# Attention with a soft cap and two MoE layers: a fixed order for three engines in the first seven pairs

## The chip, the cores and the metric

One core of a Trainium2 chip runs the kernel. The metric is the device time of one execution in microseconds. An execution of the kernel before took 789.97 us as the median of three (789.9 to 790.86). The profile comes from one further execution, which took 788.29 us.

## The reference

Three steps are chained; the output of each is the input of the next. All is float32.

```
# 1. attention: 4 batches, 12 heads, 448 positions, head size 64
s = cap * tanh((q @ k.T / 8) / cap)                     # cap = 30
p = exp(s - max(s));  attn = p / (sum(p) + 1e-9) @ v
x = attn with the heads side by side                    # 1792 tokens x 768

# 2. first "MoE" layer: w_in 768 x 1024, w_out 1024 x 768
h = x @ w_in;  e = exp(h - max(h))
solu = h * e / (sum(e) + 1e-9)
y = ((solu - mean) / sqrt(var + 1e-6) * g_ln) @ w_out

# 3. second layer: 8 experts, top 1, w1 768 x 1024 and w2 1024 x 768 for each
logits = y @ w_gate + modality_bias[modality_id]
out = gate * (relu(y @ w1[e]) @ w2[e])                  # e, gate of each token
```

`w_in` and `w_out` come to the chip as 64-bit floats and are turned into 32-bit floats there.

## The kernel before, in words

**Attention.** The heads are worked on two at a time: six pairs (`p`) in each of the four batches (`b`), 24 pairs in a row. A pair has its keys in four chunks of 112. Each pair is two **half pairs** (`cp` 0 and 1) of two chunks. For the first eight pairs (`plain`) a half pair is: scores on TensorE (`sc`, L664), a tanh and an exp of each chunk on ScalarE (`e`, L667 and L669), then the products with v (`av`, L714) and, for the first six pairs, the row sums through TensorE (`S`, L720). TensorE adds the products of a pair's first two chunks in its second half pair, and those of the last two in the first half pair of the next pair; then `av` is copied to `X` (L729). Later pairs split k and q into a high and a low part (`a_split`, L645 to L648) and use these.

**Weights of the first MoE.** While the attention of batch 0 runs, `w_in` and `w_out` are brought in and converted block by block: 12 half rows of `w_in` (128x512) and 16 of `w_out` (128x384). GpSimd issues the load of a raw block (`conv_load`, L450; four buffers, so each load waits until an earlier block has been read). VectorE turns the raw bits into float32 in three operations (`f64_to_f32`, L426 to L428). A block of `w_in` is then split into a high part on ScalarE (L463) and a low part on VectorE (L464). A block of `w_out` is multiplied by `g_ln` (`g_t`) and split on VectorE (L478, L479), transposed on TensorE (`conv_tr`, L486, copied back by ScalarE, L488), and each full row of `w_out` is multiplied by `w_gate` (`conv_og`, L494 to L496), so that the logits come out of the same product as y. The list `CUS` says in which half pair a block is due: two in each of half pairs 0 to 13. Before, all `w_in` blocks came first, then all of `w_out`.

**First MoE.** When a batch is through, its row sums are turned into reciprocals (`a_fin1`: the sums are copied from PSUM, L733, turned round by TensorE, L737, inverted by VectorE, L739 to L742, transposed back, L744, and copied to `rh`, L745 and L746), spread over the heads by products with `sel` (`a_fin2`, `rb`, L751), and multiplied onto `X` (L753). Then the token tiles of the batch are pushed onto a list of steps (`msteps`: `h` products L536 to L538, the softmax of solu, transposes, `y` products L586 to L588). `fill` takes steps from the list between the parts of each later half pair, at a pace (`pace`) that should use the list up by the time when the next batch is pushed. Each half pair has three such fills, with shares `FW` that sum to 3.

**Second layer.** Behind the attention come the routing, one expert's block as soon as its tokens are known, and the rest of the experts in slots.

**Order of the work.** TensorE's order is the order of the program text in this whole part (`manual_schedule` with TensorE alone). The order of ScalarE, VectorE, GpSimd and the DMA queue SP is chosen by the framework's planner: it takes what it expects to be ready, with the program order as the priority. Waits between engines are on semaphores, and each engine executes its own list strictly in order. The scores, transposes and gate products of this part take their PSUM tiles from one pool of three (`atile`).

Of the kernel before, what the change touches and what calls it, by code (L numbers as in the profile page):

```python
# [10 lines left out]
F32 = mybir.dt.float32  # L11
# [31 lines left out]
TAIL = (12, 12, 10)  # L43
# [6 lines left out]
NRAW = 4  # L50
NTM = 4
# [10 lines left out]
FIN = (0, 1, 2, 2)  # L62
LEFT = (6, 6, 4)
RHA = 1
BIN = 0
# [17 lines left out]
def attn_moe_kernel(ctx, tc, qt, kt, vv, cap, w_in, w_out, g_ln, ids, w_gate, mbias, w1, w2, out):  # L83
# [50 lines left out]
    def setup_tables(tp):  # L134
        flat = tp.tile([P, NP, S], F32, tag="X", name="tmp").rearrange("p a b -> p (a b)")
# [12 lines left out]
        dve.tensor_add(sel, tmp, tmp2)  # L148
# [5 lines left out]
        pool.iota(pi, pattern=[[0, 1]], base=0, channel_multiplier=1, allow_small_or_imprecise_dtypes=True)  # L154
        pi2 = tm[:, 13:14]
# [5 lines left out]
        it = tm[:, 32:60].bitcast(I32).rearrange("p (t w) -> p t w", w=2)  # L161
        sp.dma_start(out=it, in_=ids)
        mb = tm[:, 64:80].rearrange("p (t w) -> p t w", w=NE)
        sp.dma_start(out=mb, in_=mbias)
# [10 lines left out]
        sp.dma_start(out=g_t, in_=g_ln)  # L175
        sp.dma_start(out=wg_t, in_=w_gate)
        zr = flat[0:1, 2 * NP * P + 256:2 * NP * P + 256 + YW]
        dve.memset(zr, 0.0)
        sp.dma_start(out=ysc[0:1, :], in_=zr)
# [250 lines left out]
    later = {0: [], 1: [], 2: []}  # L430

    def defer(pos, f):
        if pos < 0:
            f()
        else:
            later[pos].append(f)

    def deferred(pos):
        while later[pos]:
            later[pos].pop(0)()  # L440
# [3 lines left out]
    wraw = []  # L444

    def conv_load():
        if len(wraw) < len(blocks):
# [4 lines left out]
            wraw.append(raw)  # L452

    def conv_in(k, hf):
        raw = wraw[2 * k + hf]
# [14 lines left out]
    def conv_out(c, hf):  # L470
        HW_ = DM // 2
        raw = wraw[2 * ND + 2 * c + hf]
# [7 lines left out]
        wT[c, hf] = tf  # L480

    def conv_tr(c, hf):
        tf = wT[c, hf]
        pt = atile(f"pt{c}_{hf}")[:, 0, :]
        for i in range(3):
            pe.transpose(pt[:, i * P:(i + 1) * P], tf[:, i * P:(i + 1) * P], ident)  # L486
        tt = mp.tile([P, 3, P], F32, tag="x3", name=f"wT{c}_{hf}", bufs=4)
        act.copy(tt, pt[:, :3 * P].rearrange("p (a b) -> p a b", a=3))  # L488
        wT[c, hf] = tt
# [923 lines left out]
```

## Time and profile before

| | |
|---|---|
| median of three executions | 789.97 us |
| the profiled execution | 788.29 us |
| its span, first to last instruction | 786.6 us |
| TensorE busy | 737.2 us, 94% |
| VectorE busy | 452.6 us, 58% |
| ScalarE busy | 393.7 us, 50% |
| GpSimd busy | 209.8 us, 27% |
| mean granted TensorE clock | 0.980 |

Busy times of TensorE are modelled, since its matmuls are pipelined: two neighbours overlap in the records, and the distance of their starts is the time that one of them costs. "PE" is TensorE's matmul side and "PEld" its weight loads, "DVE" is VectorE, "ACT" ScalarE, "POOL" GpSimd, "SP" the queue that issues most loads. `L664` is line 664 of the kernel before. The granted clock is 1.00 at 2.4 GHz and falls by halves of time: a mean of 0.8 means that the clock was at 1.2 GHz for 40% of the stretch.

### The profile page before, as it was taken

To read this page: it belongs to the slowest core of one execution; us is meant where nothing else is said; L and a number is where in the kernel's file an instruction comes from. 1 tells how busy PE (TensorE), PEld (TensorE's weight loads), DVE (VectorE), ACT (ScalarE), POOL (GpSimd) and SP (SyncE) were. 2 spreads that over 40 slices of the span, in tenths; PEclk is the share of its full clock that TensorE was granted. 3 is DMA by queue.
4 is the path that set the end of the run, shared out by engine and by line. 5 is a ranking of instruction groups with operands and counts; after the bars stand their busy time and mean duration, and the time that the engine had idled before them with its cause. 6 is when DMAs were issued, how large, how long until landed. Compare 5 with 4: busy or idle time off the path is not lost.

```text
span 786.6 us, 11389 instructions
## 1 busy us (share of the span) xinstructions
PE 737.2 (94%) x4150; PEld 576.3 (73%) x4150; DVE 452.6 (58%) x833; ACT 393.7 (50%) x541; POOL 209.8 (27%) x285
## 2 busy tenths in 40 slices
PE   6889899998999998999999999899999999999993
PEld 2234456776677777676868799889879988799982
DVE  5987767767656665665444745747246163463630
ACT  5987656774656554556641223525136162553530
POOL 4222015352343351336432213540300211002010
PEclk9999999999999999999999999999999999999997
DMA  9856202231313221122000402476938459574620
GB/s 299 284 178 168 90 19 82 67 109 54 102 36 102 79 69 60 57 69 79 13 21 20 142 21 91 128 277 218 362 135 251 147 173 379 199 254 166 211 79 23
DMA packets 39060, 104.50 MB, mean 133 GB/s; under 512 B 6439, under 2 KB 16689, under 8 KB 38994
## 3 DMA queue, kind: packets, MB, share of 16 engines
q1 hardware_dynamic: 32466, 74.26, 29.0%
q0 software_dynamic: 6528, 29.42, 10.8%
q8 instruction: 34, 0.56, 0.3%
q14 instruction: 32, 0.26, 0.1%
HBM read 92.58 MB, written 11.27 MB: 132 GB/s over the span
## 4 chain that ended last, share of the span: by engine, by line
PE 78%; DVE 7%; issue 6%; ACT 3%; DMA 3%; POOL 1%; SPq 0%; POOLq 0%; DVEq 0%; ACTq 0%
PE av L714 8%; PE h L536 5%; PE y L586 5%; PE h L538 5%; PE y L588 5%; PE y L587 5%; PE h L537 5%; PE sc L689 3%; PE sc L690 3%; PE poD L1160 3%; PE poD L1161 3%; PE poD L1162 3%; PE phD L1091 3%; PE phD L1092 3%; PE phD L1093 3%
## 5 line engine op out<-in xcount | busy, mean ns | idle before, releaser
L692 ACT ACTIVATE e<-sc,sc 112x896 f32<-112x896 f32 x64 | 64.6, 1009 | 83.4 <-PE sc L690 81.2
L714 PE MATMUL av<-e,v 112*64 112x448 f32 x384 | 82.0, 560 | 3.1 <-ACT e L669 2.3
L586 PE MATMUL y<-wouh,lh 128*128 128x388 f32 x224 | 77.4, 345 | 2.2 <-ACT lh L576 1.9
L588 PE MATMUL y<-wouh,ll 128*128 128x388 f32 x224 | 76.4, 341 | 0.3 <-DVE ll L577 0.2
L587 PE MATMUL y<-woul,lh 128*128 128x388 f32 x224 | 76.2, 340 | 0.0
L536 PE MATMUL h<-winh,xh 128*128 128x512 f32 x168 | 69.3, 413 | 0.1
L538 PE MATMUL h<-winh,xl 128*128 128x512 f32 x168 | 66.8, 398 | 0.9 <-POOL xl L524 0.5
L693 ACT ACTIVATE e<-e,cap_t 112x896 f32<-112x896 f32 x64 | 66.9, 1045 | 1.5
L537 PE MATMUL h<-winl,xh 128*128 128x512 f32 x168 | 66.5, 396 | 0.0
L714 PEld LDWEIGHTS av<-e,v 112*64 112x64 f32 x384 | 24.9, 140 | 53.1 <-issue 38.4
L689 PE MATMUL sc<-qs,kh 128*112 128x448 f32 x128 | 48.2, 377 | 2.3 <-DVE u L548 1.3
L701 POOL TENSOR_TENSOR es<-es,e 112x448 f32<-112x448 f32 x32 | 40.8, 1276 | 34.1 <-DVE es L700 33.5
L586 PEld LDWEIGHTS y<-wouh,lh 128*128 128x128 f32 x224 | 42.4, 189 | 8.4 <-issue 4.3
L648 POOL TENSOR_TENSOR kl<-kr,kh 128x448 fp32r<-128x448 f32 x22 | 28.3, 1288 | 75.3 <-DVE kh L645 44.9
L690 PE MATMUL sc<-qs,kl 128*112 128x448 f32 x128 | 47.7, 372 | 0.0
L1037 DVE TENSOR_TENSOR wl_H<-raw_H,wh_H 128x768 fp32r<-128x768 f32 (+1 forms) x28 | 29.2, 1068 | 29.4 <-ACT wh_H L1036 29.3
L1037 DVE TENSOR_TENSOR wl_D<-raw_D,wh_D 128x768 fp32r<-128x768 f32 (+1 forms) x28 | 29.8, 1071 | 24.6 <-ACT wh_D L1036 24.0
L588 PEld LDWEIGHTS y<-wouh,ll 128*128 128x128 f32 x224 | 42.2, 188 | 1.1 <-DVE ll L577 1.0
L587 PEld LDWEIGHTS y<-woul,lh 128*128 128x128 f32 x224 | 42.3, 189 | 0.9
L1160 PE MATMUL poD<-wh_D,hhD 128*128 128x384 f32 x128 | 43.0, 336 | 0.0
L1162 PE MATMUL poD<-wh_D,hlD 128*128 128x384 f32 x128 | 42.8, 334 | 0.0
L1161 PE MATMUL poD<-wl_D,hhD 128*128 128x384 f32 x128 | 42.8, 334 | 0.0
(382 smaller groups left out, 1769.0 us busy)
## 6 DMA issues: line engine op xcount, KB each, us to landing
kr<-in_kt_dram SPq DMA_DIRECT2D x64, 112.0 KB, 2.5
qr<-in_qt_dram SPq DMA_DIRECT2D x64, 112.0 KB, 2.6
rawc<-in_w_in_dram POOLq DMA_DIRECT2D x12, 512.0 KB, 5.8
rawc<-in_w_out_dram POOLq DMA_DIRECT2D x16, 384.0 KB, 3.8
raw_D<-in_w_dram SPq DMA_DIRECT2D x12, 512.0 KB, 3.9
wr_T<-in_w_dram SPq DMA_DIRECT2D x16, 384.0 KB, 5.7
raw_D<-in_w_dram SPq DMA_DIRECT2D x16, 384.0 KB, 4.5
wr_T<-in_w_dram SPq DMA_DIRECT2D x12, 512.0 KB, 9.0
```

The lines of the kernel that those rows point to most:

```text
L536: pe.matmul(o, s["xh"][d], winh[d][:, c], start=(d == 0), stop=False)
L537: pe.matmul(o, s["xh"][d], winl[d][:, c], start=False, stop=False)
L538: pe.matmul(o, s["xl"][d], winh[d][:, c], start=False, stop=(d == ND - 1))
L586: pe.matmul(o, s["lh"][f], wouh[f][:, c], start=(f == 0), stop=False)
L587: pe.matmul(o, s["lh"][f], woul[f][:, c], start=False, stop=False)
L588: pe.matmul(o, s["ll"][f], wouh[f][:, c], start=False, stop=(f == NF - 1))
L689: pe.matmul(ps[:CK, c, :S], kh[:, k0:k0 + CK], qs, start=True, stop=False)
L690: pe.matmul(ps[:CK, c, :S], kl[:, k0:k0 + CK], qs, start=False, stop=True)
L693: act.activation(e, e, AF.Exp, scale=cap_t[:CK])
L714: pe.matmul(o[64 * j:64 * j + 64, :S], v[:, c, 64 * j:64 * j + 64], et[b, p, j, c], start=(c == 0), stop=(c == 3))
L1160: pe.matmul(p, hh[:, f, o], wh[:, c], start=(f == 0), stop=False)
L1161: pe.matmul(p, hh[:, f, o], wl[:, c], start=False, stop=False)
```

## The change

In the first seven pairs (`FIXED`) ScalarE's and VectorE's lists follow the program text as well, beside TensorE's. For that the text of a half pair is written out anew (`unit`): scores; both tanh; the transposes and gate products that the half pair before left (`flush("pe")`); the ScalarE casts that it left (`flush("cast")`); both exp (`a_exp`, which was part of `a_scp`); the products with v; the conversion of the blocks due; the VectorE subtractions that are open (`flush("sub")`). The blocks alternate, one of `w_out` and one of `w_in` in each of half pairs 0 to 11, and two of `w_out` in half pairs 12 and 13. The transposed halves of a row of `w_out` go to one tile with one buffer (`ys`) instead of two of the four-buffer tag `x3`.

The tables for routing are set up in two parts, in half pairs 0 and 3, and the loads of `g_ln` and `w_gate` are issued before the raw blocks.

The end of a batch is spread: the copy of the row sums follows the last product of the batch (`a_ssb`), `a_sums` and `a_recip` take the place of `a_fin1`. `FIN` now counts quarters: `finish` is called in the middle and at the end of a half pair. The sums stand in the middle of half pair 1 of the next batch, the transposes of the reciprocals at its end, the three `rb` products in the middle and (twice) at the end of half pair 2; before, the sums and transposes stood at the end of half pair 0, the `rb` products at the ends of half pairs 1, 2 and 2. The push of the tiles stays at the end of half pair 2, and the pace counts 27 parts and `LEFT` from there, where it counted 30. At the end of the last batch `TAIL` has a fourth number, for the steps left when the reciprocals are transposed.

```diff
-TAIL = (12, 12, 10)
+TAIL = (14, 12, 12, 10)
+FIXED = 7
-FIN = (0, 1, 2, 2)
+FIN = (2, 3, 4, 5, 5)
...
-    blocks = [(w_in, 512, k, h) for k in range(ND) for h in range(2)] + \
-        [(w_out, DM // 2, c, h) for c in range(NF) for h in range(2)]
+    blocks = []
+    for i in range(2 * NF):
+        blocks.append((w_out, DM // 2, *divmod(i, 2)))
+        if i < 2 * ND:
+            blocks.append((w_in, 512, *divmod(i, 2)))
...
-        def rest():
+        def cast():
             act.copy(h_, tf)
-            dve.tensor_sub(l_, tf, h_)
-
-        defer(BIN, rest)
+            later["sub"].append(lambda: dve.tensor_sub(l_, tf, h_))
+
+        later["cast"].append(cast)
...
     def conv_out(c, hf):
...
         wT[c, hf] = tf
+        later["pe"].append(lambda: conv_tr(c, hf))
...
     def conv_tr(c, hf):
...
+        act.copy(wT[c][:, 3 * hf:3 * hf + 3, :], pt[:, :3 * P].rearrange("p (a b) -> p a b", a=3))
+        if hf:
+            later["pe"].append(lambda: conv_og(c))
...
-    def a_fin1(b):
+            if p == NP - 1:
+                a_ssb(b)
+
+    def a_ssb(b):
         ssb = ap_.tile([P, S], F32, tag="es", name=f"ssb{b}", bufs=5)
         act.copy(ssb, spt[b][:, :S])
...
+    def a_sums(b):
+        ssb, po = sums[b], atile(f"sum{b}")
...
+    def a_recip(b):
+        r, po = sums.pop(b), atile(f"rt{b}")
...
         if u == FIN[0]:
-            a_fin1(b)
+            a_sums(b)
+        if u == FIN[1]:
+            a_recip(b)
         for q in range(3):
-            if u == FIN[q + 1]:
+            if u == FIN[q + 2]:
                 a_fin2(b, q)
...
-            pace(3 * (2 * NP - FIN[3]) + LEFT[b])
+            pace(3 * (2 * NP - (FIN[4] + 1) // 2) + LEFT[b])
...
+    def unit(n, cp):
+        (b, p), u = pairs[n], 2 * n + cp
+        if plain(b, p):
+            a_scp(b, p, cp)
+            flush("pe")
+            flush("cast")
+            a_exp(b, p, cp)
+        else:
+            a_sc(b, p, 0, cp)
+            flush("pe")
+            flush("cast")
+        if cp == 0 and n:
+            a_av(*pairs[n - 1], chunks=(2, 3) if plain(*pairs[n - 1]) else range(4))
+        elif cp and plain(b, p):
+            a_av(b, p, chunks=(0, 1))
+        fill(FW[0])
+        if b > 0:
+            finish(b - 1, 4 * p + 2 * cp)
+        while convs and CUS[crate[0]] <= u:
+            crate[0] += 1
+            convs.pop(0)()
+        flush("sub")
+        if u == 0:
+            tables.append(setup_first(flat))
+        if u == 3:
+            setup_second(*tables[0])
+        a_esp(b, p, cp)
...
+        if b > 0:
+            finish(b - 1, 4 * p + 2 * cp + 1)
...
+    with tc.manual_schedule(engines={ET.PE, ET.Activation, ET.DVE}):
         a_load(*pairs[0])
-        a_split(*pairs[0])
         v_load(*pairs[0])
         a_load(*pairs[1])
+        sp.dma_start(out=g_t, in_=g_ln)
+        sp.dma_start(out=wg_t, in_=w_gate)
         for _ in range(4):
             conv_load()
...
+        for n in range(FIXED):
+            unit(n, 0)
+            unit(n, 1)
+    with tc.manual_schedule(engines={ET.PE}):
+        for n in range(FIXED, len(pairs)):
+            unit(n, 0)
+            unit(n, 1)
         a_av(B - 1, NP - 1)
         fill(2)
-        a_fin1(B - 1)
+        a_sums(B - 1)
+        while len(msteps) > TAIL[0]:
+            msteps.pop(0)[1]()
+        a_recip(B - 1)
```

## Rows read from the trace of the kernel before

**Rows 1.** Page: busy us, share of span, instructions of each engine.

```profile
PE 737.2 (94%) x4150; PEld 576.3 (73%) x4150; DVE 452.6 (58%) x833; ACT 393.7 (50%) x541; POOL 209.8 (27%) x285
```

**Rows 2.** Windows: stretch, length, busy us (instructions) by engine, granted clock, DMA share.

```profile
7.85:45.57 37.72, 31.73 (x156) 9.67 (x156) 31.75 (x67) 32.77 (x41) 8.05 (x14) 0.99 0.89 298
45.57:74.04 28.47, 26.89 (x169) 13.84 (x169) 21.75 (x47) 23.65 (x35) 6.30 (x10) 0.96 0.54 161
74.04:102.44 28.40, 25.19 (x148) 13.54 (x147) 20.39 (x48) 18.45 (x29) 2.24 (x3) 0.88 0.35 97
...
184.00:190.00 6.00, 3.00 (x16) 2.63 (x17) 4.72 (x12) 1.34 (x4) 2.11 (x6) 0.82 0.01 1
...
212.00:300.00 88.00, 88.00 (x459) 66.87 (x458) 51.98 (x90) 48.95 (x61) 34.74 (x39) 1.00 0.25 75
300.00:308.00 8.00, 6.51 (x32) 5.49 (x31) 5.25 (x11) 3.77 (x7) 1.17 (x1) 0.79 0.00 1
```

**Rows 3.** Timeline of TensorE, opening: start, us, engine, line, operation, shapes, idle before.

```profile
7.85 6.21 PE L664 MATMUL sc<-qr,kr 64*112 64x448 f32 x16 [7.85 <-DMA qr<-in_qt_dram]
...
16.53 1.76 PE L664 MATMUL sc<-qr,kr 64*112 64x448 f32 x8
...
20.77 1.76 PE L664 MATMUL sc<-qr,kr 64*112 64x448 f32 x8
...
44.76 0.88 PE L486 MATMUL pt<-ident,to 128*128 128x128 f32 x3 [2.92 <-DVE to L428]
...
50.97 0.87 PE L486 MATMUL pt<-ident,to 128*128 128x128 f32 x6
...
53.01 1.76 PE L664 MATMUL sc<-qr,kr 64*112 64x448 f32 x8
...
102.44 3.25 PE L664 MATMUL sc<-qr,kr 64*112 64x448 f32 x8
...
107.43 1.08 PE L751 MATMUL rb<-rh,sel 128*128 128x448 f32 x4
...
111.88 0.50 PE L536 MATMUL h<-winh,xh 128*128 128x512 f32 x1
```

**Rows 4.** TensorE's waits, 103 to 400 us: for whom, us in total, times, longest.

```profile
PE sum L744 <- DVE rr L742: 3.6, 2, 2.1
PE sum L737 <- ACT ssb L733: 1.5, 1, 1.5
```

**Rows 5.** Timeline of VectorE: a w_in and a w_out block, tables, sums, X.

```profile
16.91 0.43 DVE L426 TENSOR_SCALAR ti<-rawc 128x512 int32<-128x512 int32 x1
...
18.71 0.68 DVE L464 TENSOR_TENSOR winl<-ti,winh 128x512 fp32r<-128x512 f32 x1
19.31 0.95 DVE L148 TENSOR_TENSOR sel<-tmp 128x768 fp32r<-128x768 f32 x1
...
46.78 0.62 DVE L479 SCALAR_TENSOR_TENSOR woul<-to,g_t,wouh 128x384 fp32r<-128x384 f32 x1
...
49.35 0.62 DVE L479 SCALAR_TENSOR_TENSOR woul<-to,g_t,wouh 128x384 fp32r<-128x384 f32 x1
...
97.59 1.15 DVE L682 TENSOR_TENSOR es<-es,e 112x448 f32<-112x448 f32 x2
...
102.55 1.09 DVE L753 TENSOR_TENSOR X<-X,rb 128x896 f32<-128x896 f32 x1
...
409.44 0.27 DVE L740 TENSOR_SCALAR rr<-sum,epsv 112x48 f32<-112x48 f32 x1 [0.51 <-PE sum L737]
...
410.23 0.19 DVE L742 COPY rr<-rr 112x48 f32<-112x48 f32 x1
```

**Rows 6.** DMA issues: KB, median us to landing; and SP's queue at 3.62 us.

```profile
rawc<-in_w_in_dram POOLq DMA_DIRECT2D x12, 512.0 KB, 5.8
g_t<-in_g_ln_dram SPq DMA_DIRECT2D x1, 4.0 KB, 9.1
...
3.62 0.90 SPq L162 DMA_DIRECT2D tmp<-in_ids_dram  x1
```

More of the change, by code (lines that the diff above doesn't have):

```diff
@@ L428, in f64_to_f32, with flush @@
         dve.scalar_tensor_tensor(dst, lo, 29, dst, op0=ALU.logical_shift_right, op1=ALU.bitwise_or)
-    later = {0: [], 1: [], 2: []}
-    def defer(pos, f):
-        if pos < 0:
-            f()
[L435 to L440, printed above, removed]
-    blocks = [(w_in, 512, k, h) for k in range(ND) for h in range(2)] + \
-        [(w_out, DM // 2, c, h) for c in range(NF) for h in range(2)]
-    wraw = []
+    later = {"pe": [], "cast": [], "sub": []}
+    def flush(kind):
+        fs, later[kind] = later[kind], []
+        for f in fs:
+            f()
+    blocks = []
[3 more added lines that the diff above has]
+            blocks.append((w_in, 512, *divmod(i, 2)))
+    wraw, rawof = [], {}
     def conv_load():
@@ L452, in conv_load @@
             wraw.append(raw)
+            rawof[src is w_in, k, h] = raw
     def conv_in(k, hf):
-        raw = wraw[2 * k + hf]
+        raw = rawof[True, k, hf]
         t = mp.tile([P, 512], I32, tag="x3", name=f"ti{k}_{hf}", bufs=4)
@@ L493, in conv_og @@
         for i in range(ND):
[L494 removed]
+            pe.matmul(po[:, :NE], wT[c][:, i, :], wg_t[:, i, :], start=(i == 0), stop=(i == ND - 1))
         act.activation(wouh[c][:, DM:YW], po[:, :NE], AF.Copy, scale=g_t[:, c:c + 1])
[L496 to L497 removed]
+        later["sub"].append(lambda: dve.scalar_tensor_tensor(
+            woul[c][:, DM:YW], po[:, :NE], g_t[:, c:c + 1], wouh[c][:, DM:YW], op0=ALU.mult, op1=ALU.subtract))
     rpool = []
@@ L654, in e_new @@
         return ap_.tile([CK, 2, S], F32, tag="e", name=nm, bufs=5)
+    exps = {}
     def a_scp(b, p, cp):
@@ L667, in a_scp, with a_exp @@
             act.activation(e, t[:CK, :, :S], AF.Tanh, scale=sc8[:CK])
-        for c, e in zip(chunks, es):
+        exps[b, p, cp] = es
+    def a_exp(b, p, cp):
+        for c, e in zip((2 * cp, 2 * cp + 1), exps.pop((b, p, cp))):
             act.activation(e, e, AF.Exp, scale=cap_t[:CK])
@@ L761, in attn_moe_kernel @@
     crate = [0]
-    convs = [(1, lambda k=k, h=h: conv_in(k, h)) for k in range(ND) for h in range(2)]
-    for i in range(2 * NF + 2):
-        if i < 2 * NF:
-            convs.append((1, lambda c=i // 2, h=i % 2: conv_out(c, h)))
-        if 0 < i <= 2 * NF:
-            convs.append((0, lambda c=(i - 1) // 2, h=(i - 1) % 2: conv_tr(c, h)))
-        if i > 1 and i % 2 == 1:
-            convs.append((0, lambda c=(i - 3) // 2: conv_og(c)))
+    convs = [lambda f=conv_in if src is w_in else conv_out, k=k, h=h: f(k, h) for src, _, k, h in blocks]
     msteps, drained = [], set()
@@ L822, in finish @@
                     push_tile(t)
-            pace(3 * (2 * NP - FIN[3]) + LEFT[b])
-    with tc.manual_schedule(engines={mybir.EngineType.PE}):
+            pace(3 * (2 * NP - (FIN[4] + 1) // 2) + LEFT[b])
[26 more added lines that the diff above has]
+        a_esp(b, p, cp)
+        if cp == 0 and n + 1 < len(pairs):
+            a_split(*pairs[n + 1], js=(0,))
+        if not plain(b, p):
+            a_sc(b, p, 1, cp)
+        fill(FW[1])
+        if cp == 1 and n + 1 < len(pairs):
+            a_split(*pairs[n + 1], js=(1,))
+        if cp == 1 and n + 2 < len(pairs):
+            a_load(*pairs[n + 2])
+        if cp == 0 and n + 1 < len(pairs):
+            v_load(*pairs[n + 1])
+        fill(FW[2])
+        if b > 0:
+            finish(b - 1, 4 * p + 2 * cp + 1)
@@ L871, in attn_moe_kernel @@
         for q in range(3):
-            while len(msteps) > TAIL[q]:
+            while len(msteps) > TAIL[q + 1]:
                 msteps.pop(0)[1]()
```

74 lines of the change are left out of this document (21 added, 53 removed).

## The prediction

> **What bounds the kernel now.** I read the page first: TensorE is busy 94% of the span [rows 1]. A mean over stages says little, so I cut the span into stretches, each at a start that the timeline of TensorE shows. From the first tile of the first MoE on, TensorE is full: 88.00 of 88 us between 212 and 300, at the full clock [rows 2]. Work removed from another engine there is worth nothing; what starts there earlier ends earlier. Two places are different.
>
> The first is the opening, seven pairs of heads, 14 half pairs. Scores of half pair 0 start at 7.85 us, those of half pair 14 at 102.44, and the first product of the MoE ("h") at 111.88 [rows 3]: 94.6 us for 14 half pairs, 6.76 each. Over the three stretches that make up this time TensorE has 31.73 + 26.89 + 25.19 = 83.8 us of work, partly at half clock, VectorE 73.9 and ScalarE 74.9 [rows 2]. So none of the three is full, and they wait for each other in turns. The reader is to see the case at 44.76: TensorE has stood still for 2.92 us until VectorE had converted a block of w_out; after that its clock is low, as in the scores at 102.44, 3.25 us for eight matmuls that take 1.76 at 16.53 [rows 3].
>
> The second place is the end of each batch: TensorE issues the sums and at once the transposes of the reciprocals, and waits between them for VectorE, 3.6 us in two batches, besides 1.5 us for ScalarE's copy of the sums [rows 4]. The clock is 0.82 over the 6 us at the first of these and 0.79 over the 8 us at the second [rows 2].
>
> **The change part by part.** *TensorE in the opening.* A half pair without weights is 20.77 - 16.53 = 4.24 us; a row of w_out (two transposes and the gate product) is 53.01 - 50.97 = 2.04 us, 1.02 in each half pair, since the blocks of w_out now come one by one [rows 3]. That is 5.26, at full clock, and 14 of them 73.6: TensorE alone could be at half pair 14 at 81.5.
>
> *ScalarE.* Its work does not change: 74.9 / 14 = 5.35 by durations [rows 2]. The new order puts both tanh first, then the copies and casts, then both exp, so no operation follows the one whose result it needs; neighbours then overlap a little and it is nearer 5. It loses the work for pair 8 that stood in this stretch, which comes back behind half pair 14, beside TensorE.
>
> *VectorE* now runs each block's chain without anything in between. One block of w_out, five dependent operations, is 49.35 - 46.78 = 2.57; the three conversions of a w_in block 18.71 - 16.91 = 1.80; its subtraction 19.31 - 18.71 = 0.60 [rows 5]. With the small gate subtraction of every second half pair that is 5.05 in a half pair with one block of each. So three engines need 5.26, about 5 and 5.05: balanced, and 1.5 below today's 6.76. Before, the twelve w_in blocks came first, so that no w_out work reached TensorE until 44.76; afterwards each half pair carried two w_out blocks.
>
> The order is tied together with half a pair of slack in each place: the transposes, casts and exps of a half pair use what the half pair before left. I therefore add up VectorE's own list, which has the most extra work:
> - Start. The first block now is w_out and needs g_t. g_t's load goes out behind five bulk loads, at about the 3.62 us where the load of ids stood; it took 9.1 us to land [rows 6]. I take 3.6 + 9.1 = 12.7. VectorE waits there, with three conversions (1.6 us) done ahead; at today's place it would be idle until 7.5 anyhow. Bounds: 9 us, if it passes the bulk, and 14.4, today's landing.
> - Half pair 0 from there: 1.0 for the rest of the block, 1.8 for w_in, 1.9 for three memsets of the tables: 17.4.
> - Half pairs 1 to 11: 11 x 5.05 = 55.6, and 2.7 for the second half of the tables in half pair 3 (the 0.95 addition [rows 5] and a dozen small operations): 75.7.
> - Half pair 12: two w_out blocks 5.1, one w_in subtraction 0.6, two additions of exps 1.15 [rows 5]: 82.6.
> - Half pair 13: the sums of batch 0. VectorE reaches them before TensorE, which must have the second w_out block of half pair 12 (converted at about 80), then a transpose, the products with v and the sums; TensorE is done at about 85, a wait of 2.4. Reciprocals 1.0, from 409.44 to the end of the last at 410.42 [rows 5]; two w_out blocks 5.1; four additions 2.4; the subtraction on rh 0.6: 94.1.
>
> TensorE, ahead by then, waits in half pair 14 for rh; then the three pairs of rb products take about 1, and the scores, the last gate product and the products with v of half pair 15 about 4.7, where today 4.45 lie between 107.43 and 111.88 [rows 3]. The multiplications of X (1.09 each [rows 5]) lie beside them. First h at 99.8 instead of 111.88: **12.1 us earlier**. Bounds: 88.5, if TensorE never waits (81.5, then two half pairs of 4.24 with their weights and rb, less a wait); 109, if it does its 5.26 at the clock of 0.82 to 0.88 that rows 2 have and all waits stay.
>
> *Loads.* A raw block's buffer is freed by the third conversion and refilled for the half pair after next: about 8.5 us to spare, against a landing of 5.8 for w_in [rows 6] and 0.6 of issue. Cost nothing; the cover is 2 us, and a landing beyond 8.5 would stop VectorE. The setup's affine selections move on POOL behind the first refills; nothing needs their result before half pair 3. The loads of ids and bias move behind g_t on SP, and are needed there as well.
>
> *Batch ends 1 and 2.* ssb is copied in the half pair before, the sums stand in the middle of half pair 1, the reciprocals' transposes at its end, with filled-in MoE work between: VectorE's chain of 1.0 and its queue are covered. That removes 3.6 + 1.5 us [rows 4] and the time at low clock: a mean of 0.82 over 6 us is 2.2 us at half speed, 0.79 over 8 us 3.4, and at half speed half of it is lost, 1.1 + 1.7 [rows 2]. Gross 7.9. What is late next: rb of the first third moves half a half pair later, close to the other two, and the pacing counts 33 parts instead of 36, so that MoE work of the last batch runs out a half pair earlier. At the push of the new tiles TensorE then has only scores, 0.8, and waits for two multiplications of X at 1.09 [rows 5], a cast and VectorE's queue. I charge 2 us per batch, bounds 0 and 5 (with the clock). Net **-3.9**, between -7.9 and +2.
>
> *Last batch.* By the pacing (31 parts, 29 used before the sums, 15.2 weight for each of three tiles) some 2.7 of weight are left, six or seven steps; the new bound of 14 steps pops none, so the wait for the reciprocals stays. 0.
>
> Sum against the profiled execution's own 788.29 (span 786.6): 788.3 - 12.1 - 3.9 = 772.3. The median of the runs stands 1.7 above that execution; the forecast in terms of the median is **774.0**. Behind 112 us I find nothing that hangs on absolute time: TensorE has the same work and is full.
>
> **The clock, weighed.** The profile shows a fall after a 2.92 us idle stretch [rows 3], and a stretch with 6 us of scattered idle time at 0.99, the first of rows 2. By these rows short waits leave the clock at 2.4 GHz, and I charged none. The Trainium skill, page "TensorE: Matmul & The Clock Gate", section "HAM oscillation — how this bites in real kernels", says that a loop whose turn is shorter than the wait in it can fall back to the low clock in every turn; here the loop is the half pair. Its price in rows is the first rival. This trace agrees with the page from 74 us on (0.88), and not in the first stretch.
>
> **Rivals.**
> 1. *The clock stays low in the opening.* TensorE's 5.26 become 6 to 6.6 by the granted 0.82 to 0.88 and it sets the pace: 14 x 6.3 = 88, half pair 14 at 98, first h at 107 to 109. Saving 3 to 5, and 3.9 at the ends: about 782. For it: TensorE waits in hand order too. Against: it needs 5.26 of about 5.5, and the old low stretches follow long waits. Chance 0.15.
> 2. *VectorE does better than its list.* If g_t passes the bulk (9 us) and the sums do not wait, TensorE is the bound: first h at 90 to 93, about 765 with the ends. For it: 4 KB only. Against: every small load at that place took 9 to 10 us. Chance 0.10.
> 3. *Hand order turns into lockstep (slower).* An engine with a fixed order cannot step round an operation that waits. VectorE's last operation of a half pair waits for ScalarE's cast of that half pair, which stands behind two tanh and a copy, itself behind TensorE's transpose. If the half pair of slack is used up, the half pair becomes VectorE's 4.4 up to there, ScalarE's 2.7 and 0.6 more: 7.7 instead of 6.76, 14 x 0.94 = 13.2 later; with -3.9 at the ends 788.3 + 9.3 + 1.7 = 799. It is slower from a half pair of 6.76 + 3.9 / 14 = 7.04 on. For it: the planner needed 6.76 with free choice. Against: the slack is written into the order, and 5.05 to 5.35 leave 1.4. Chance 0.11.
> 4. *Gained and given back.* The opening gains less than half, since POOL refills or PSUM tiles (three, of which the gate product holds one until late in VectorE's list) stop it, and the batch ends give +2: 785 to 790. Chance 0.09.
>
> **How the numbers follow.** The forecast, 768 to 779 by half of each bound, has 0.55. Low end 764: the second rival and the better half of the bounds. High end 787: the first rival and most of the fourth. Outside lie the third and a little of the second and fourth, about 0.18. Below 0.2% (1.6 us) a measurement of this kernel tells nothing. Faster: 0.55 + 0.15 + 0.10 + half of the fourth, 0.84. Same: 0.04. Slower: the third and a crumb, 0.12.
>
> **What would show it.** In the changed kernel: half pair 14's scores near 87 and the first h near 100 on TensorE; half pairs of 5 to 5.5; VectorE's first wait in half pair 0 for g_t, at 12 to 13; no TensorE wait over 3 us between 20 and 80, and a clock near 1.00 there; no wait of "sum" for "rr" in batches 1 and 2, and a new one of h for X or xh at their pushes; from there to the end the old distances. Wrong would be: half pairs above 6, TensorE waiting in each for a PSUM tile or ScalarE, or a first h that comes early while the end does not follow.

## The result, and the profile after

The changed kernel takes 783.58 us (median of 10 runs, 779.1 to 786.63); the kernel before, run beside it, 790.41 (10 runs). The ratio is 0.9901, with an interval of 0.9876 to 0.9926: 1.0% faster, where 2.0% was forecast. The time lies inside the range that was given (764 to 787), but the change is less than half of the forecast: 6.8 us by the two medians, 7.8 by the ratio, instead of 12.1 + 3.9 = 16.0. The profiled execution took 781.89 us, its span is 780.1.

The page has as many instructions on the four compute engines as before [rows 1]; VectorE's take 5.7 us longer in all, some of them drawn out as its timeline shows below:

```profile
PE 736.0 (94%) x4150; PEld 575.8 (74%) x4150; DVE 458.3 (59%) x833; ACT 390.1 (50%) x541; POOL 210.3 (27%) x285
```

The windows of the changed kernel, cut at the scores of half pairs 0, 3, 9, 13 and 14, at the first h and at the first rb of the last batch (columns as in rows 2):

```profile
6.94:28.13 21.19, 15.25 (x63) 5.22 (x63) 13.39 (x24) 12.95 (x16) 7.31 (x10) 0.84 0.77 248
28.13:61.89 33.76, 32.49 (x203) 13.53 (x199) 32.34 (x70) 30.48 (x43) 7.47 (x13) 1.00 0.71 222
61.89:84.98 23.09, 21.95 (x137) 9.00 (x133) 22.23 (x40) 21.04 (x33) 6.38 (x9) 1.00 0.73 219
84.98:93.51 8.53, 7.13 (x50) 4.26 (x47) 6.77 (x16) 6.64 (x11) 0.00 (x0) 1.00 0.40 116
93.51:111.98 18.47, 15.17 (x69) 7.31 (x68) 16.75 (x33) 10.33 (x15) 1.22 (x1) 0.85 0.06 15
111.98:415.77 303.79, 298.32 (x1529) 224.09 (x1528) 187.20 (x319) 174.31 (x226) 122.25 (x174) 0.99 0.22 66
```

The second line is what the change was to make of the whole opening: TensorE and VectorE are both busy for 96% of it, at 2.4 GHz, and a half pair takes 33.76 / 6 = 5.6 us. The first and the fifth line give it back. The scores of half pair 14 start at 93.51, 9 us earlier than before [rows 3], but the first h at 111.98, where it was. The whole gain lies behind it: from the first h to the first rb of the last batch 303.8 us, before 311.5 (111.88 to 423.42); the rest of the span took 1.2 us longer in these two executions.

TensorE's timeline in the two bad stretches, as in rows 3. (Half pairs 0 and 1 have their scores together from 6.90 on; those at 15.02 are half pair 2's.)

```profile
15.02 1.76 PE L669 MATMUL sc<-qr,kr 64*112 64x448 f32 x8
22.71 0.87 PE L487 MATMUL pt<-ident,to 128*128 128x128 f32 x3 [5.94 <-DVE to L428]
23.52 3.26 PE L722 MATMUL av<-e,v 112*64 112x448 f32 x8
...
93.04 0.54 PE L763 MATMUL rt<-ident,rr 112*44 112x112 f32 x4 [1.16 <-DVE rr L757]
93.51 1.01 PE L669 MATMUL sc<-qr,kr 64*112 64x448 f32 x4
95.63 1.01 PE L669 MATMUL sc<-qr,kr 64*112 64x448 f32 x4 [1.11 <-ACT e L672]
98.21 1.56 PE L497 MATMUL po<-wg_t,wT 128*128 128x8 f32 x12 [1.57 <-DVE woul L499]
...
101.22 2.55 PE L722 MATMUL av<-e,v 112*64 112x448 f32 x8
103.70 1.49 PE L770 MATMUL rb<-rh,sel 128*128 128x448 f32 x6
...
109.25 2.80 PE L722 MATMUL av<-e,v 112*64 112x448 f32 x8
111.98 0.80 PE L539 MATMUL h<-winh,xh 128*128 128x512 f32 x1
```

VectorE's timeline, to be read against the prediction's list for it (rows 5 have operations of the same kind at their old lengths):

```profile
14.81 0.42 DVE L478 TENSOR_SCALAR wouh<-to,g_t 128x384 fp32r<-128x384 f32 x1 [7.07 <-DMA g_t<-in_g_ln_dram]
...
20.02 0.28 DVE L426 TENSOR_SCALAR to<-rawc 128x384 int32<-128x384 int32 x1
21.47 1.10 DVE L428 SCALAR_TENSOR_TENSOR to<-rawc,to 128x384 int32<-128x384 int32 x1
...
71.46 1.94 DVE L479 SCALAR_TENSOR_TENSOR woul<-to,g_t,wouh 128x384 fp32r<-128x384 f32 x1
...
81.48 1.57 DVE L426 TENSOR_SCALAR to<-rawc 128x384 int32<-128x384 int32 x1
...
91.92 0.27 DVE L755 TENSOR_SCALAR rr<-sum,epsv 112x48 f32<-112x48 f32 x1 [1.49 <-PE sum L752]
...
97.94 0.22 DVE L499 SCALAR_TENSOR_TENSOR woul<-po,g_t,wouh 128x8 fp32r<-128x8 f32 x1
...
100.90 0.62 DVE L765 TENSOR_TENSOR rh<-rt,rh 12x448 fp32r<-12x448 f32 x1
```

Where TensorE waits between 111 and 400 us, as in rows 4: "sum" no longer waits for "rr" or "ssb", and the new waits at the two pushes of tiles are 1.2 us of rb for X (at 199), 1.5 of h for xh and 0.2 for xl.

```profile
PE h L539 <- ACT xh L526: 1.5, 1, 1.5
PE rb L770 <- DVE X L772: 1.2, 1, 1.2
...
PE h L541 <- DVE xl L527: 0.2, 1, 0.2
```

### The profile page after: what moved, and what is told of

The parts are those of the page before. It is cut to its first block, busy times and chain, and to the rows that moved or that the text cites. A ratio compares the mean times of both kernels' runs of the same rounds, so it can differ in the third digit from the quotient of the medians.

```text
span 780.1 us, 11377 instructions
## 1 busy us (share of the span) xinstructions
PE 736.0 (94%) x4150; PEld 575.8 (74%) x4150; DVE 458.3 (59%) x833; ACT 390.1 (50%) x541; POOL 210.3 (27%) x285
## 4 chain that ended last, share of the span: by engine, by line
PE 77%; DVE 11%; issue 4%; ACT 3%; DMA 3%; SPq 0%; POOL 0%; POOLq 0%; ACTq 0%; DVEq 0%
PE av L722 7%; PE h L539 5%; PE h L541 5%; PE h L540 5%; PE y L589 5%; PE y L591 5%; PE y L590 5%; PE sc L697 3%; PE sc L698 3%; PE poD L1199 3%; PE poD L1201 3%; PE poD L1200 3%; PE phD L1130 3%; PE phD L1131 3%; PE phD L1132 3%
## 5 line engine op out<-in xcount | busy, mean ns | idle before, releaser
L651 POOL TENSOR_TENSOR kl<-kr,kh 128x448 fp32r<-128x448 f32 x22 | 26.6, 1208 | 66.6 <-DVE kh L648 50.8
L539 PEld LDWEIGHTS h<-winh,xh 128*128 128x128 f32 x168 | 32.0, 190 | 15.2 <-issue 5.8
```

What stands on the lines that cost most here:

```text
L539: pe.matmul(o, s["xh"][d], winh[d][:, c], start=(d == 0), stop=False)
```

## The experiments

Each version ran beside the kernel before on the same chip, but not all versions on one chip; so versions are compared by their ratios to the kernel before, and two ratios differ clearly only where their intervals do not overlap. "first h" and "half pair 14" are starts on TensorE in the profiled execution.

### Which part gives the gain

**e2_ends_only**: the kernel before with only the spread batch ends.

```diff
-TAIL = (12, 12, 10)
+TAIL = (14, 12, 12, 10)
-FIN = (0, 1, 2, 2)
+FIN = (2, 3, 4, 5, 5)
+            if p == NP - 1:
+                a_ssb(b)
...
-            pace(3 * (2 * NP - FIN[3]) + LEFT[b])
+            pace(3 * (2 * NP - (FIN[4] + 1) // 2) + LEFT[b])
```

> The kernel before, with the batch ends alone spread as in the change (sums in the middle of half pair 1, transposes at its end, rb in half pair 2, the pace counted from there); the opening stays the planner's. Theory A (the first h stands at 111.98 against 111.88, so the opening is worth nothing and all of the gain lies at the ends): 6 to 8 us under the kernel before, 782 to 784. Theory B (the opening has also helped, in what it leaves to the planner behind 112 us): 2 to 4 us under it.

**e3_open_only**: the changed kernel with the old ends and the old pace.

```diff
-FIN = (2, 3, 4, 5, 5)
+FIN = (1, 1, 3, 5, 5)
-TAIL = (14, 12, 12, 10)
+TAIL = (999, 12, 12, 10)
...
-            if p == NP - 1:
-                a_ssb(b)
...
     def a_sums(b):
+        a_ssb(b)
...
-            pace(3 * (2 * NP - (FIN[4] + 1) // 2) + LEFT[b])
+            pace(3 * (2 * NP - 2) + LEFT[b])
```

> The changed kernel, with the batch ends as before: sums and transposes of the reciprocals together at the end of half pair 0, rb at the ends of half pairs 1, 2 and 2, the pace counted as before; the fixed opening stays. Theory A: the same as the kernel before within 2 us, with waits of sum for rr and ssb back in batches 1 and 2. Theory B: 3 to 5 us under the kernel before.

**e4_pace36**: the changed kernel with the pace alone as before.

> The changed kernel with the pace counted over 36 parts as before instead of 33, so that the MoE steps of the batch before reach into half pair 2, where the rb products and the push of the next tiles stand. If it is the shorter pace that leaves TensorE without work at the push (waits of h for xh 1.5 us and of rb for X 1.2 us in the changed kernel), they go, and the time is 1 to 3 us lower. If the shorter pace helps, since it does MoE steps early that otherwise are left for the last batch's end (there the rb products come 7.7 us earlier in the changed kernel, the last products with v only 3.4), the time is the same or up to 2 us higher.

Measured:

- e2: 781.36 us, ratio 0.9883 (0.9849 to 0.9917). The ends alone give 9 us, more than either theory had; the first h stands at 112.15, where it was.
- e3: 793.28 us, ratio 1.0022 (0.9998 to 1.0046): Theory A, the opening alone gives nothing in the time. Its first h is at 110.41, 1.5 us earlier than before.
- e4: 786.61 us, ratio 0.9933 (0.9909 to 0.9956). The two waits at the push go, as expected, but TensorE waits 2.5 us elsewhere (scores for VectorE's work on `sm`, the small sums of solu) and 1.0 for rr, and the time is higher: the second theory. Its profiled execution, 790.99, is the slowest of its eleven.

From e3 to e4 only the ends are spread: 6.7 us by the medians of one chip, intervals apart. From e4 to the changed kernel only the pace is shorter: 2.5 us by the two ratios (0.9933 - 0.9901 of 790), but these intervals overlap. The traces agree with both: from the first h to the last batch's first rb it is 312.3 us in e3, 305.4 in e4 and 303.8 in the changed kernel. Together that is e2's gain. The waits of e3 show what comes back with the old ends (same view as above):

```profile
PE rt L762 <- DVE rr L756: 3.8, 2, 2.2
PE sum L751 <- ACT ssb L743: 1.5, 1, 1.5
```

### What the opening lost at its start and in the middle

**e1_g_first**: g_ln's load is SP's first.

```diff
+        sp.dma_start(out=g_t, in_=g_ln)
         a_load(*pairs[0])
...
         a_load(*pairs[1])
-        sp.dma_start(out=g_t, in_=g_ln)
```

> The changed kernel, with g_t's load issued as the first of SP's loads instead of behind five bulk loads. In the changed kernel VectorE stands still for 7.07 us in half pair 0 until g_t lands at 14.8 us. Theory A (VectorE's own list carries the opening, so a wait at its head moves everything behind it): VectorE goes on at 8 to 9, the first h comes 5 to 7 us earlier, at 105 to 107, and the time is 5 to 7 us under the changed kernel's, about 777. Theory B (the two half pairs behind the fixed part set the end of the opening; TensorE and the planner's list there take up what comes earlier): half pair 14 starts earlier, but the first h moves by less than 2 us and so does the time.

Measured: 777.54 us, ratio 0.9832 (0.9796 to 0.9867), 5.5 us below the changed kernel by the ratios: Theory A in the time. In the opening it lies between the two: half pair 4 starts at 26.68 instead of 34.18, 7.5 us earlier, half pair 14 at 90.28, 3.2 earlier, and the first h at 108.99, 3.0 earlier. The DMA issues (KB, us to landing) and ScalarE's timeline in the middle:

```profile
g_t<-in_g_ln_dram SPq DMA_DIRECT2D x1, 4.0 KB, 1.7
```

```profile
64.39 0.56 ACT L648 CAST kh<-kr 128x448 fp32r<-128x448 f32 x1 [2.33 <-DMA kr<-in_kt_dram]
64.86 1.00 ACT L672 ACTIVATE e<-sc,sc 112x896 f32<-112x896 f32 x1
65.76 0.55 ACT L649 CAST qs<-qr 128x448 fp32r<-128x448 f32 x1
66.22 1.01 ACT L672 ACTIVATE e<-sc,sc 112x896 f32<-112x896 f32 x1
```

The 4 KB land after 1.7 us there, and VectorE uses them at 7.51. In the changed kernel they were issued at 3.61, behind five bulk loads of their queue and beside four raw blocks that GpSimd had issued, and VectorE could go on at 14.81, 11.2 us later. The second fence shows casts that split pair 8 before each of the two tanh of half pair 10. ScalarE's order is fixed only for the instructions of the seven pairs; the split of pair 8 is issued outside, and the planner put it forward, into their midst, where it waits for kr and ScalarE with it. The changed kernel has the same two casts at 69.84 and 71.22.

**e5_fixed8** fixes eight pairs on top of this, **e6_early_setup** moves the first half of the tables ahead of half pair 0, **e7_fixed8_early** does both, and **e8_light** leaves out the third conversion of the last four blocks of w_out in e7.

```diff
-FIXED = 7
+FIXED = 8
```

```diff
+        tables.append(setup_first(flat))
         for n in range(FIXED):
...
-        if u == 0:
-            tables.append(setup_first(flat))
```

> The load of g_ln first (as in e1_g_first) and eight pairs in hand order instead of seven, so that the split of pair 8 stands behind half pair 13 in ScalarE's list as well. e1_g_first had its scores of half pair 11 at 66.28, those of half pair 14 at 90.28, the first h at 108.99 and a median of 777.54 us. Theory A (the planner's placing of pair 8's casts between the tanh of half pairs 10 to 13 costs the wait of 2.33 us for kr and the half clock behind it): half pairs 11 to 13 of 5.0 to 5.5, scores of half pair 14 at 83 to 85, the first h at 104 to 106, median 773 to 775. Theory B (VectorE's list of half pairs 12 to 15, with two blocks of w_out each, the sums and the reciprocals, sets the first h whatever ScalarE does): scores of half pair 14 earlier by 3 or more, the first h still at 108 to 109, median 777 to 778.

> As e1_g_first, with the first part of the routing tables set up ahead of half pair 0 instead of at its end: three memsets leave VectorE's list of the loop (2.1 us), and GpSimd's affine selections end before VectorE's blocks of half pair 1. Theory A (VectorE's list sets the pace from the start, and GpSimd's selections cost VectorE 1.6 us there): half pair 4's scores at 23 to 24 instead of 26.68, the first h 3 to 4 earlier than 108.99, median near 774. Theory B (TensorE and ScalarE set the steady half pairs, and the place lost at half pairs 9 to 12 takes back what is gained): half pair 4 earlier, the first h within 1 us of 108.99, median 777 to 778.

> Both edits, e5_fixed8 and e6_early_setup. Theory A: they add, the first h at 101 to 103, median 769 to 772. Theory B (one bound behind half pair 11, VectorE's list): the first h at 105 to 109 and a median not below that of the better of the two by more than 1.

> As e7_fixed8_early, but for the last four blocks of w_out the third conversion, which brings in the low word, is left out: four VectorE operations of 0.56 us less in half pairs 12 and 13, 2.3 us with their gaps; the lowest bits of a quarter of w_out are not computed. If VectorE's list sets the time from half pair 12 to the first h: the first h 2 to 2.5 earlier than in e7_fixed8_early, median 2 lower. If TensorE or ScalarE sets it: within 0.5 us of e7_fixed8_early in both.

Measured:

- e5: 777.64 us (ratio 0.9849, 0.9816 to 0.9881), half pair 14 at 85.53 instead of 90.28, first h at 108.40: Theory B. Of the 4.8 us, 4.2 are lost again behind half pair 14.
- e6: 775.08 (0.9809, 0.978 to 0.9839), first h at 106.60, 2.4 earlier than in e1 and so between the theories, nearer A. Half pair 4 is no earlier (28.46), as the products with v ahead of it ran at half clock (3.09 us for eight).
- e7: 775.81 (0.9834, 0.9791 to 0.9877), half pair 14 at 83.30, first h at 106.18: Theory B.
- e8: 778.91 (0.9853, 0.9821 to 0.9885), first h at 105.40: 0.8 for 2.3 us of VectorE's work, so its list is not the only bound there. Its median is above e7's, inside the two intervals, and its profiled execution took 2.8 us longer behind the last batch's first rb, which nothing in the edit explains.

### The stretch behind half pair 14

In e7 TensorE takes 22.9 us from half pair 14 to the first h. Its timeline and VectorE's:

```profile
83.30 1.01 PE L669 MATMUL sc<-qr,kr 64*112 64x448 f32 x4
85.42 1.83 PE L669 MATMUL sc<-qr,kr 64*112 64x448 f32 x4 [1.11 <-ACT e L672]
88.00 2.73 PE L497 MATMUL po<-wg_t,wT 128*128 128x8 f32 x12 [0.75 <-DVE woul L499]
...
92.92 3.26 PE L722 MATMUL av<-e,v 112*64 112x448 f32 x8
```

```profile
81.70 0.27 DVE L755 TENSOR_SCALAR rr<-sum,epsv 112x48 f32<-112x48 f32 x1 [4.33 <-PE sum L752]
...
87.73 0.22 DVE L499 SCALAR_TENSOR_TENSOR woul<-po,g_t,wouh 128x8 fp32r<-128x8 f32 x1
...
90.44 0.62 DVE L765 TENSOR_TENSOR rh<-rt,rh 12x448 fp32r<-12x448 f32 x1
```

VectorE waits 4.33 us for the sums, then converts two blocks, and only then reads the gate product (87.73) and the transposed reciprocals (90.44). Each holds one of the three PSUM tiles until then, so the two chunks of scores of half pair 14 must share the third, and the second four matmuls wait 1.11 us for the tanh of the first. (In e10, where both tiles are given back early, the eight run without a wait: 1.76 us from 84.72.) Two edits act on this, alone in the changed kernel (**e9_after_tiles**) and in e7 (**e10_tiles**, **e11_blocks_first**, **e12_both**):

```diff
+        if c >= 5:
+            pg = mp.tile([P, NE], F32, tag="pg", name=f"pg{c}", bufs=3)
+            act.activation(pg, po[:, :NE], AF.Copy, scale=g_t[:, c:c + 1])
+            later["sub"].append(lambda: dve.tensor_sub(woul[c][:, DM:YW], pg, wouh[c][:, DM:YW]))
...
-        dve.tensor_sub(rh[32:HR], po[32:HR, 1, :S], rh[32:HR])
+        src = po[:, 1, :S]
+        if b == 0:
...
+            act.copy(src[32:HR], po[32:HR, 1, :S])
+        dve.tensor_sub(rh[32:HR], src[32:HR], rh[32:HR])
```

```diff
-        if b > 0:
-            finish(b - 1, 4 * p + 2 * cp)
         while convs and CUS[crate[0]] <= u:
             crate[0] += 1
             convs.pop(0)()
+        if b > 0:
+            finish(b - 1, 4 * p + 2 * cp)
```

> The changed kernel, with two PSUM tiles given back early at the end of the opening: ScalarE copies the last three gate products and batch 0's transposed reciprocals from PSUM (0.27 and 0.5 us each), and VectorE subtracts from the copies. In the changed kernel VectorE reads these two of the three tiles only at 97.94 and 100.90 us, behind two blocks of w_out, and TensorE waits in half pair 14 (1.11 for ScalarE, 1.57 for VectorE) and falls to half clock; from half pair 14 to the first h it takes 18.5 us. Theory A (the held tiles are what stops TensorE there): no wait for L499, half pair 14 to the first h in 14 to 16.5 us, median 2 to 4 below 783. Theory B (VectorE's list itself is late, rh comes at 100.9 anyhow): the waits move to rb, the stretch stays at 17.5 us or more, median within 1.5 of 783.

> The same two copies in e7_fixed8_early, where half pair 14 starts at 83.3 and the first h at 106.18. Theory A: half pair 15 follows after 9 to 11 us instead of 15.7, the first h at 100 to 102, median 770 to 772. Theory B: the first h at 104.5 or later.

> e7_fixed8_early with the blocks of a half pair ahead of the sums in the program text: VectorE converts the two blocks of half pair 13 in the 4.33 us in which it waited for the sums at 77.4 to 81.7, and reads the sums, the gate product and the reciprocals 4 us earlier. The tiles are then free earlier without a copy. Theory A (late reads of VectorE hold the tiles and the reciprocals): half pair 14 to 15 in 10 to 12 us instead of 15.7, the first h at 101 to 103, median 770 to 772. Rival: TensorE waits for the reciprocals in half pair 13 as much longer as it waits less in 14: the first h at 105 to 106.5.

> Both, in e7_fixed8_early. If the tiles and VectorE's wait for the sums are two names for one loss, the first h is where the better of e10_tiles and e11_blocks_first has it, within 1 us; if they add, 2 to 4 earlier than either, near 98 to 100, about where the prediction had put it, median 767 to 770.

Measured:

- e9: 783.06 us (ratio 0.9886, 0.9862 to 0.991), half pair 14 to first h 18.5 us: Theory B in the numbers, the tiles alone are worth nothing in the changed kernel. But it is not rh that holds TensorE: rh is ready at 101.24, and TensorE comes to rb only at 103.21, at a granted clock of 0.78 over the stretch (the eight scores take 3.02 us, the products with v 3.25), and waits for `X` behind it (0.92 and 0.66).
- e10: 773.18 (0.9758, 0.9732 to 0.9783), first h at 104.42: nearly Theory B. Its wait is now for rh:

```profile
93.46 2.41 PE L779 MATMUL rb<-rh,sel 128*128 128x448 f32 x6 [3.02 <-DVE rh L774]
```

- e11: 773.11 (0.9777, 0.9751 to 0.9804), half pair 15 after 10.0 us, first h at 102.53: Theory A, with a median 1 us above it.
- e12: 770.89 (0.9739, 0.9718 to 0.976), first h at 102.89: one loss under two names in the place of the first h. Its median is 2.2 lower than either's, which the intervals do not separate.

Of the versions without idle work e12 has the lowest time, 1.6% below the changed kernel. In it VectorE is done with rh at 87.95, 4.6 us before TensorE uses it, and yet half pair 14 to the first h takes 17.5 us, at a low clock:

```profile
84.92 0.54 PE L768 MATMUL rt<-ident,rr 112*44 112x112 f32 x4 [1.94 <-DVE woul L502]
85.39 3.04 PE L674 MATMUL sc<-qr,kr 64*112 64x448 f32 x8
...
96.55 1.01 PE L674 MATMUL sc<-qr,kr 64*112 64x448 f32 x4 [1.11 <-ACT e L677]
98.16 1.64 PE L497 MATMUL po<-wg_t,wT 128*128 128x8 f32 x12 [0.60 <-DVE X L781]
99.73 3.23 PE L727 MATMUL av<-e,v 112*64 112x448 f32 x8
```

```profile
85.40:102.89 17.49, 15.36 (x70) 7.64 (x69) 9.52 (x16) 12.22 (x21) 1.13 (x1) 0.80 0.15 41
```

### Does one wait bring the clock down?

**e13_dummy** and **e15_full** put products that nothing reads behind the sums of batch 0 in e12; **e14_late** moves the transposes of its reciprocals half a half pair back.

```diff
+        if b == 0:
+            k, q = raws[1, 0]
+            for j in range(8):
+                pe.matmul(po[:CK, 1, :S], k[:64, :CK], q[:64], start=True, stop=True)
```

```diff
+        if b == 0:
+            for j in range(5):
+                pe.matmul(po[:, 1, :S], winh[0][:, :P], winh[0][:, 512:512 + S], start=True, stop=True)
```

```diff
+        FIN = (2, 4, 5, 5, 5) if b == 0 else (2, 3, 4, 5, 5)
```

> e12_both with eight products of 64x112x448 (0.22 us each, 1.76 together) behind the sums of batch 0 in TensorE's order; nothing reads them. In e12_both TensorE waits 1.94 us there before the transposes of the reciprocals, and the scores of half pair 14 behind it take 3.04 us for eight that take 1.76 at full clock; from half pair 14 at 85.39 to the first h it takes 17.5 us at a granted clock of 0.80. Theory A (this wait brings the clock down, and the low clock is what the last stretch loses): the wait below 0.4, those scores in 1.8, the stretch in 14 to 15.5 us, the first h at 99.5 to 101, median 2 below e12_both's 770.89. Theory B (the clock falls in this stretch whatever fills that one wait, since half pairs 14 and 15 have waits of their own, 1.11, 0.60 and 0.43): the stretch at 16.5 to 17.5, the median within 1 of 770.9.

> e12_both with the transposes of batch 0's reciprocals in the middle of half pair 14 instead of the end of 13, so that scores, a gate product and products with v stand between the sums and them; the three rb products follow at the end of half pair 14. The wait of 1.94 goes; TensorE then waits for the two copies and the subtraction of the reciprocals, about 1.7 us, before rb. Theory A (the clock falls at the wait, wherever it is): half pair 14 starts at 83.5 and its scores take 1.8 us, the low clock begins behind 90 instead of 85, the first h 1 to 3 earlier than 102.89. Theory B (the wait is only moved and the clock falls as before): the first h within 1 of 102.89, median within 1 of 770.9.

> e12_both with five products of 128x128x448 from the first MoE's converted w_in (about 0.37 us each at full clock, 1.8 together) behind the sums of batch 0, in place of e13_dummy's 64-row products, which took 9.95 us and at the end of which the clock was at 0.50 all the same; nothing reads them. Theory A (the wait of 1.94 brings the clock down): the five take 1.8 to 2, the wait for the reciprocals is below 0.4, the scores of half pair 14 take 1.8 instead of 3.04, the first h at 100 to 101.5, median 769 to 770. Theory B (the clock falls in this stretch anyway): the scores of half pair 14 or the products with v behind them at half clock again, the first h within 1 us of 102.89, median within 1 of 770.9.

Measured: e13 775.20 us (ratio 0.9796, 0.9757 to 0.9835). Its eight products stand as 16 records in the trace and took 9.95 us instead of 1.76, and the clock fell while they ran, so it doesn't test Theory A:

```profile
81.30:83.80 2.50, 2.50 (x9) 1.26 (x9) 0.90 (x3) 0.00 (x0) 0.00 (x0) 0.99 0.00 0
83.80:86.30 2.50, 2.50 (x5) 1.06 (x4) 0.00 (x0) 0.00 (x0) 0.00 (x0) 0.50 0.00 0
```

e14 771.98 (0.9753, 0.9717 to 0.9789), first h at 102.65: Theory B, with a median 1.1 us above e12's. The place of the low clock moved with the wait, as Theory A has it: scores of half pair 14 start at 82.72 and take 1.76, but TensorE then waits 1.99 for rh and 2.39 for X, and those of half pair 15 take 3.33. e15 770.30 (0.973, 0.9715 to 0.9744), first h at 103.89: Theory B too, but the edit didn't remove the wait. The five products took 1.25 us, VectorE reads the sums behind them, and TensorE's wait was 1.16; the scores behind it took 3.01.

What this stretch takes without such waits can be read in e3, which was run for another end. There the old end of batch 0 has its sums and reciprocals in half pair 12, and VectorE makes rh (at 91.30) before the two blocks of half pair 13, not behind them:

```profile
98.05 1.76 PE L669 MATMUL sc<-qr,kr 64*112 64x448 f32 x8
100.17 1.50 PE L497 MATMUL po<-wg_t,wT 128*128 128x8 f32 x12 [0.36 <-ACT e L672]
...
102.61 1.72 PE L722 MATMUL av<-e,v 112*64 112x448 f32 x8
...
110.41 0.51 PE L539 MATMUL h<-winh,xh 128*128 128x512 f32 x1
```

From half pair 14 at 98.05 to the first h it is 12.4 us, with one wait of 0.36 us, at a granted clock of 1.00; the changed kernel takes 18.5 us there for nearly the same matmuls (69 records, 68 in e3). e3 pays earlier instead: from the sums at 85.93 to half pair 14 it takes 12.1 us at a granted clock of 0.72, with waits of 1.85 for ssb and 2.70 for rr. No run with the fixed opening has the end of batch 0 without a wait in either place; what that would give stays open.

## Why the prediction was wrong

**The term that failed is the opening, "First h at 99.8 instead of 111.88: 12.1 us earlier"; measured +0.1.** It lies outside the bounds given for it (88.5 to 109). It was added up on VectorE's list, and by that list it can be taken apart (predicted ends 17.4, 75.7, 82.6, 94.1, 99.8):

| part of the list | predicted | measured | off by |
|---|---|---|---|
| up to the end of half pair 0 | 17.4 | 20.0 | +2.6 |
| half pairs 1 to 11 | 58.3 | 61.5 (20.02 to 81.48) | +3.2 |
| half pair 12 | 6.9 | 8.7 (to 90.2) | +1.8 |
| half pair 13, to the end of rh | 11.5 | 11.3 (to 101.5) | -0.2 |
| from rh to the first h | 5.7 | 10.5 (to 111.98) | +4.8 |

On TensorE the same 12.2 us are 6.5 up to half pair 14 (at 93.51, not near 87) and 5.7 behind it (18.5 us to the first h, not 12.8).

- *Start.* g_t was put at 12.7, by adding the 9.1 us that its load took before to an earlier issue. The trace of before has the issue at 5.26 and so the landing at 14.4; issued at 3.61, 1.65 us earlier, the data came no earlier, at 14.8. Over the four executions with the load in this place VectorE got it at 13.00 (e9), 13.06 (e3), 14.81 and 15.21 (e4): the landing behind the bulk is not a constant. Issuing it first gave 5.5 us.
- *Half pairs 1 to 11.* The count of 5.05 a half pair is right where nothing else runs: VectorE's turns of half pairs 4 to 9 are 4.96 to 5.13. Not counted were two meetings. "The setup's affine selections move on POOL ...; nothing needs their result" is true of their result, but while four of them run (18.56 to 23.30) VectorE's two-operand conversions take 1.09 and 1.10 instead of 0.56. And pair 8's split, which I let "come back behind half pair 14", stands at half pairs 10 to 12, by the planner's choice: L650 on VectorE twice (74.50 and 85.65), and GpSimd's subtraction beside L479 (1.94 instead of 0.62) and L426 (1.57 instead of 0.35).
- *The last stretch.* I had TensorE ahead of VectorE there, waiting for rh, and at full clock. It was neither: the products with v of half pair 14 came only at 101.22, after the two waits for PSUM tiles (1.11 and 1.57), and rb at 103.70, 2.2 us after rh was done; at a granted clock of 0.85 about 5.5 of 18.5 us ran at 1.2 GHz, up to half of them lost. The tiles, which the prediction named only in its fourth rival, hold TensorE but are worth nothing alone in the changed kernel (e9). With g_t early, eight pairs fixed and the tables ahead (e7), the tiles give 1.8 us of the first h (e10), the blocks ahead of the sums 3.7 (e11), both 3.3 (e12).

The edits for these causes together, in e12, bring the first h from 111.98 to 102.89: 9.1 of the 12.2 us missing. The rest lies in the last stretch, 17.5 us where 12.8 was predicted.

**The batch ends gave more than predicted: -3.9 forecast, 9 measured alone (e2).** The mechanism held: the waits for rr and ssb are gone. Of the gross 7.9, 6.7 came (e3 to e4). The step that failed is the charge of 2 us per batch, for the push and the shorter pace. At the two pushes 2.9 us of waits stand, where 4 was charged (rb for X, h for xh and xl). The shorter pace cost nothing: waits of 3.7 us that the kernel before has elsewhere between 111 and 400 us (scores and transposes for `u`, the softmax of solu, scores for `ys`, a tile of y, and h for xl) are gone but for that 0.2 for xl, while e4, with the old pace, still has 2.4 of them. By the ratios the pace gains 2.5, which is not clear of the noise. The bound of -7.9 was too narrow by a little. The last batch's wait for the reciprocals stayed, as predicted (1.2 us). So it is in part luck that the time lies inside the range: one term failed by 12 us, and the other, beyond its own bound, made up for 5.

**Clock.** From half pair 3 through half pair 13 the clock was 1.00 with seven waits of 0.16 to 1.16 us; so the first rival did not come, and the page of the Trainium skill that it stood by ("TensorE: Matmul & The Clock Gate", section "HAM oscillation — how this bites in real kernels") describes a case that this loop did not become: less work than wait in each turn. Nor was the 0.88 of rows 2 from 74 us on that case, as the prediction had it: half pairs there have 4 us of work or more and waits of 1.69 at most. Half pair 14 of the changed kernel does look like it: work of 1.01 us and waits of 1.11 and 1.57 in turns, at a granted clock of 0.85 from there to the first h. The prediction's reading that short waits leave the clock at 2.4 GHz did not hold, and no length of a wait tells the cases here apart. In e6 the eight products with v behind a wait of 0.73 us took 3.09 (clock 0.58 from 24 to 28 us), in e1 those behind a wait of 1.10 took 1.72 (clock 1.00). What brings the clock down in these stretches stays open.

**Rivals.** The second's first condition, g_t at 9 us or earlier, was made true by e1 (7.51): the first h came at 108.99, not at 90 to 93. The fourth (gained and given back, 785 to 790) was nearest in mechanism, but wrong about where: the ends did not lose, they carried all of it. Lockstep did not occur; steady half pairs took 5.6.

## What to carry to other kernels

An order written by hand fixes only the instructions inside it: look where the planner puts those just outside (fixing one pair more brought half pair 14 4.8 us forward in e5, though not yet the time). How long a load took at one place in a queue says little for another place: issue the small load that the first work needs ahead of the bulk. Where one engine's list sets the pace, count everything on the engine next to it that may slow it, and let it do the short steps that others wait for, shared PSUM tiles and the sums of a batch, before its long work, not after. At the end of a pipelined stage with nothing to fill it, count each hand-over both ways and at the low clock.

## What the runs showed of the hardware

- VectorE and GpSimd slow each other when they work at the same time. GpSimd's timeline in the changed kernel has two equal selections at 0.87 (from 18.56) and, as VectorE's two-operand operations start, 1.64; and the subtraction that meets L479:

```profile
18.56 0.87 POOL L137 TENSOR_SCALAR_AFFINE_SELECT tmp<-tmp 128x768 f32<-128x768 f32 x1
19.39 1.64 POOL L143 TENSOR_SCALAR_AFFINE_SELECT tmp<-tmp 128x768 f32<-128x768 f32 x1
...
71.82 1.16 POOL L651 TENSOR_TENSOR kl<-kr,kh 128x448 fp32r<-128x448 f32 x1
```

  The Trainium skill, page "SBUF — State Buffer", section "Who interferes with whom", says that a VectorE operation with two SBUF inputs contends with a GpSimd one that reads SBUF, and that the order of issue decides which of the two is blocked. The trace agrees that they contend: 1.94 us for L479 is its own 0.62 and 1.32 more, about one subtraction of GpSimd (1.16). The order of the records does not show the second part: L479 began at 71.46, before the subtraction, and was the one drawn out. Operations with one tensor input were slowed as well: L478 took 0.90 instead of 0.42 beside a selection, L426 1.57 instead of 0.35 beside a subtraction.
- A load of 4 KB took 1.7 us to land as the first of its queue (e1). Issued behind five bulk loads, on none of which it depends, its data could be used 9.4 to 11.6 us after its issue (four executions).
- TensorE's clock fell from 2.4 to 1.2 GHz while its records lay without a gap: in e13 with products that use 64 rows and 112 columns, one at a time (0.54 us for each of their records at first, 0.95 behind the fall). Scores of the same shape, two beside each other in the records, ran at a granted clock of 1.00 in half pairs 3 to 13 of the changed kernel.
